# RWKV-5 attention into a top-1 mixture of experts: moving a count, an early block and the first load

## The chip, the cores and the metric

The kernel runs on one core of one Trainium2 chip. The metric is device microseconds for one execution. Before the change three executions took 365.10, 365.97 and 366.94 us; the median is 365.97 us. One more execution was taken with the hardware profiler on; it took 372.31 us, of which 370.4 us lie between its first and last instruction (the span). Every duration and waiting time below is from that execution.

## The reference

Two blocks follow each other. The first is a linear-attention recurrence (RWKV-5) over batch 4, 8 heads, 768 tokens and head width 48, with a decay `w` and a bonus `u` for each channel:

```
for t in range(S):
    cur = outer(u * k[t], v[t])
    y[t] = r[t] @ (state + cur)
    state = w[:, None] * state + outer(k[t], v[t])
```

The second takes the 3072 tokens of width 384 that result and sends each to one of 8 experts:

```
logits = x @ w_gate;  e = argmax(logits);  g = max of softmax(logits)
out = g * (relu(x @ w1[e]) @ w2[e])          # w1: 384 x 1024, w2: 1024 x 384
```

All values are float32.

## The kernel before

**Turns.** The attention works on pairs of heads: 4 batches of 4 pairs make 16 turns (`U`), numbered 0 to 15. In a turn the 768 tokens stand as 6 chunks (`G`) of 128 (`C`). r and k of a pair (`rk`) lie with the channels on 112 partitions, v and k once more (`vk`) with the tokens on 128. The instructions of every engine stand in the order in which the code records them; no scheduler moves them.

**A turn on TensorE.** `p_own` multiplies r by k by `u` for each token (into the tile `dsb`), `p_scores` makes the scores within the chunks (into `X`), `p_tr` transposes the outputs of the turn two before, `p_ds` makes each chunk's contribution to the state (also into `dsb`), and `p_out` of the turn before applies scores and states to v (into `yps`).

**A turn on the other engines.** VectorE turns the own terms round (`own_t`, line 295), scales r and k of the next pair by the decays (`scale`, line 272, into `RK`), masks the scores (`mask`) and carries the state over the chunks (`scan`, line 331). ScalarE writes the own terms on the diagonals of the score tiles (`diag`) and empties PSUM (`out_t`, line 356, into `yT`; `keep`, lines 369 and 370, into `xb`). POOL (GpSimd) multiplies r by k of the next pair (`pairs`, line 278, into `rp`) and k by its decay (`keys`), and sends finished tokens to their experts' rows in HBM by indirect DMAs (`send`, line 418). SP issues the loads; its queue takes them in order.

**Ahead of turn 1.** Pairs 0 to 2 are loaded at once. r and k of pair 0 come in one DMA of 112 partitions (line 95), are scaled in one instruction, multiplied in `pairs(0)` on VectorE, and only then come `p_own(0)` and what hangs on it. TensorE fills its waiting time with products of the identity that nobody reads (`p_fill`, line 115): 17 at the very start and 8 ahead of turn 1. A float32 product is two records in the profile.

**The count.** From turn 5 on, `choose`, `p_rank` and `slots` find the experts and places of a finished batch's tokens. In turn 12 `p_count` (line 429) adds up the tokens of each expert so far, as one small product into `dsb`; `count` (line 432) and a compare (line 752) then check that the first two experts have at least 160 tokens (`EARLY`). Before the change they stand between `p_own` and `own_t`, and between `own_t` and `scale`.

**After the last turn.** The first 160 rows of experts 0 and 1 (`early`) need no more of the last batch. Their first layer, `L1` (line 485), is eight blocks of three products; each is followed on ScalarE by a relu and, where `then` names one, by the issue of a weight load. Blocks of `early[0]` stand between the remaining steps of turns 14 and 15: two blocks, then `p_tr(14)`, `p_out(15)`, one block, `p_tr(15)` and `keep(15)`, `choose` of the last batch, three blocks, `p_rank` of the last batch (lines 391 to 394), and then the rest without a break. After that come the late passes over all experts, which load their rows only when the last tokens have been sent.

Of the kernel before, what the change touches and what calls it, by code (L numbers as in the profile page):

```python
# [13 lines left out]
ALU = mybir.AluOpType  # L14
# [4 lines left out]
B, H, S, D = 4, 8, 768, 48  # L19
# [4 lines left out]
C = 128  # L24
G = S // C
# [4 lines left out]
KP = 64 + D  # L30
# [6 lines left out]
EARLY = 160  # L37
# [3 lines left out]
def bc(ap, shape):  # L41
    return ap.to_broadcast(shape)


def straight(tc, rk, vk, w, w1, w2, out, flag):
# [8 lines left out]
    nc = tc.nc  # L54
# [8 lines left out]
    X01 = [pp.tile([128, 4, C], FP32, name=f"X{i}") for i in range(2)]  # L63
    X23 = pp.tile([128, 2, 512], FP32, name="X23")
    yps = [pp.tile([128, 512], FP32, name=f"yps{k}") for k in range(2)]
# [5 lines left out]
    hbank = [X01[0].rearrange("p a b -> p (a b)"), X23[:, 0, :], X01[1].rearrange("p a b -> p (a b)"), X23[:, 1, :]]  # L71
# [16 lines left out]
    rks = [ca.tile([128, 2, S], FP32, name=f"rk{i}") for i in range(3)]  # L88
    vks = [ca.tile([128, 2 * G - 1, 2 * D], FP32, name=f"vk{i}") for i in range(4)]

    def load_rk(i):
        if i < U:
            b, hp = divmod(i, HP)
            if i < 3:
                nc.sync.dma_start(rks[i % 3][0:KP], rk[b, hp].rearrange("h p u s -> (h p) u s")[0:KP])
            else:

                for h in range(2):
                    nc.sync.dma_start(rks[i % 3][64 * h:64 * h + D], rk[b, hp, h, 0:D])

    def load_vk(i):
        if i < U:
            b, hp = divmod(i, HP)
            nc.sync.dma_start(vks[i % 4], vk[b, hp])
# [7 lines left out]
    def p_fill(n, o):  # L112

        for _ in range(n):
            nc.tensor.matmul(o, lhsT=ident, rhs=ident, start=True, stop=True, skip_group_check=True)
# [8 lines left out]
        nc.sync.dma_start(rows.rearrange("(e n) c -> e (n c)", e=E)[e:e + 2, PAD * HP * Q:CAP * HP * Q].rearrange(  # L124
            "e (p z) -> p e z", p=128), bc(zt[:, None, :], [128, 2, nz]))

    p_fill(17, X01[1][:, 0, :])
    strict = cp.tile([128, C], FP32, name="strict")
    nc.gpsimd.memset(strict, 1.0)
    nc.gpsimd.affine_select(out=strict, in_=strict, pattern=[[1, C]], base=-1, channel_multiplier=-1,  # L130
# [4 lines left out]
    TT = cp.tile([KP, HP, 2, C], FP32, name="TT")  # L135
# [11 lines left out]
    def decays(h0, nh):  # L147


        m = C // 2  # L150
        nc.gpsimd.memset(two(h0, nh, m, C + m - 1, 1), 1.0)
        for l in range(7):
            nc.gpsimd.tensor_tensor(pw[:, l + 1, :], pw[:, l, :], pw[:, l, :], op=ALU.mult)
        for l in range(6):
            n = 1 << l
            nc.vector.tensor_tensor(two(h0, nh, m + n, C + m - 2 * n, n), two(h0, nh, m, C + m - n, n),
                                    bc(pw[:, l, h0:h0 + nh, None, None], [KP, nh, 2, n]), op=ALU.mult)
        nc.vector.reciprocal(inv, pw[:, 6, :])
        nc.vector.tensor_tensor(two(h0, nh, 0, C + m, m), two(h0, nh, m, C, m),
                                bc(inv[:, h0:h0 + nh, None, None], [KP, nh, 2, m]), op=ALU.mult)  # L160
# [23 lines left out]
    def state_decay():  # L184
        nc.gpsimd.memset(dec, 0.0)
        nc.gpsimd.tensor_copy(dec[:, :, :, 1:], bc(pw[:, 7, :, None, None], [KP, HP, D, G - 2]))
# [55 lines left out]
    cnt2 = cp.tile([128, E], FP32, name="cnt2")  # L242
# [5 lines left out]
    viol = cp.tile([128, 24], FP32, name="viol")  # L248


    RKs = [ca.tile([128, 2, S], FP32, name=f"RK{i}") for i in range(3)]
# [15 lines left out]

        return c + 4 * h if c < 4 else 8 + 2 * h + c - 4

    def scale(i):  # L270
        hp, x = i % HP, rks[i % 3]
        nc.vector.tensor_tensor(RKs[i % 3][0:KP].rearrange("p u (c t) -> p u c t", t=C),  # L272
                                x[0:KP].rearrange("p u (c t) -> p u c t", t=C),
                                bc(TT[:, hp, :, None, :], [KP, 2, G, C]), op=ALU.mult)

    def pairs(i, eng=None):
        x = rks[i % 3]
        (eng or nc.gpsimd).tensor_tensor(rps[i % 2][0:KP], x[0:KP, 0], x[0:KP, 1], op=ALU.mult)  # L278
# [6 lines left out]
    def p_own(i):  # L285


        hp = i % HP
        x = rps[i % 2][0:KP].rearrange("p (c a j) -> p a c j", a=4, j=32)
        for a in range(4):  # L290
            nc.tensor.matmul(dsb[32 * a:32 * a + 2, 240:240 + 32 * G].rearrange("p (c j) -> p c j", j=32),
                             lhsT=ubs[:, hp, :], rhs=x[:, a], start=True, stop=True, skip_group_check=True)

    def own_t(i):
        nc.vector.transpose(own[i % 2].rearrange("p c m -> p (c m)"), dsb[:, 240:240 + 32 * G])  # L295

    def p_scores(i, cs):
        r = RKs[i % 3]
        for c in cs:
            for h in range(2):  # L300
                q = slice(64 * h, 64 * h + D)
                o = X01[h][:, c, :] if c < 4 else X23[:, h, (c - 4) * C:(c - 3) * C]
                nc.tensor.matmul(o, lhsT=r[q, 1, c * C:(c + 1) * C], rhs=r[q, 0, c * C:(c + 1) * C],  # L303
                                 start=True, stop=True, skip_group_check=True)
# [24 lines left out]
    def scan(i):  # L329
        hp = i % HP  # L330
        nc.vector.tensor_tensor_scan(Ss[i % 2][0:KP].rearrange("p e g -> p (e g)"),
                                     dec[:, hp].rearrange("p e g -> p (e g)"), dsb[0:KP, 0:240], 0.0,
                                     ALU.mult, ALU.add)
# [33 lines left out]
    def keep(i):  # L367
        b, hp = divmod(i, HP)
        nc.scalar.copy(xbs[b % 3][:, 0:4, hp, :], trv[0])
        nc.scalar.copy(xbs[b % 3][:, 4:G, hp, :], trv[1])  # L370
# [26 lines left out]
    def slots(b):  # L397
        oh, xb = ohs[b % 2], xbs[b % 3]
        nc.vector.tensor_tensor(rko, rp, oh, op=ALU.mult)
        with nc.allow_low_precision("whole numbers below 2^24"):  # L400
            nc.vector.tensor_reduce(slot[b % 2], rko, axis=AX, op=ALU.add)
# [26 lines left out]
    def p_count():  # L428
        nc.tensor.matmul(dsb[:, 480:480 + E], lhsT=ones, rhs=osum, start=True, stop=True, skip_group_check=True)

    def count(dst):
        nc.vector.tensor_tensor(dst, dsb[:, 480:480 + E], basef, op=ALU.subtract)
# [267 lines left out]
    early = [Pass(e, 0, EARLY, 0, early_bufs[e]) for e in range(2)]  # L700
# [8 lines left out]

    selection()  # L710
    decays(0, HP)
    scale(0)
    pairs(0, nc.vector)
    key_decay(0, HP)
    state_decay()
    p_scores(0, range(2))
    p_own(0)
    own_t(0)
    p_key_decay(0, 1)
# [16 lines left out]
    mask(0, 1)  # L736
    p_scores(0, range(4, G))
    mask(0, 2)
    p_fill(8, yps[0][:, 384:512])
    load_vk(3)  # L740
    for i in range(1, U):
        b, k = divmod(i - 6, 4)
        rt = i >= 6 and k == 0 and b < B - 1
        if i == 1:
            load_rk(4)
        p_own(i)
        if i == 12:
            p_count()
        own_t(i)
        if i == 12:  # L750
            count(cnt2)
            nc.vector.tensor_scalar(out=viol[:, 12:14], in0=cnt2[:, 0:2], scalar1=float(EARLY), scalar2=None, op0=ALU.is_lt)
        if i > 1:
            nc.gpsimd.tensor_copy(turn, own[i % 2][0:1, 0, 0:1])
        behind = i > 6 and i % 4 == 3
        p_scores(i, range(4 if behind else G))
        if i + 1 < U:
            scale(i + 1)
            if i == 1:
                nc.gpsimd.tensor_copy(turn, RKs[2][0:1, 0, 0:1])  # L760
            pairs(i + 1)
            load_rk(i + 4)
            keys(i + 1, nc.vector if i in (7, 8, 11, 12) else None)
        if i == 3:
            numbers()
        if i == 5:
            more_numbers()
        diag(i)
        mask(i, 0)
        mask(i, 1)  # L770
        if 2 <= i:
            p_tr(i - 2)
        p_ds(i)
        if rt:
            p_rank(b)
            slots(b)
        scan(i)
        if behind:
            p_scores(i, range(4, G))
        if rt:  # L780
            mask(i, 2)
        if 2 <= i:
            keep(i - 2)
        if not rt:
            mask(i, 2)
        if i == U - 1:
            for p in early:
                p.xT()
        if rt:
            gates(b)  # L790
            total(b, nc.gpsimd)
            ids(b)
        if i in sends:
            send(*sends[i])
        p_out(i - 1)
        out_t(i - 1)
        if i % 4 == 1 and i > 4:
            choose((i - 5) // 4)
        load_vk(i + 3)
        if 2 <= i < 6:  # L800
            clear(2 * i - 4)
        if i == 12:
            weights1(0, (0, 1))
        if i == 13:
            for p in early:
                p.load()
        if i == 14:
            weights1(0, (2, 3))


    ends = [hbank[k] for k in (0, 2, 0, 2)]
# [4 lines left out]
    send(B - 2, range(3, G))  # L816
    p_out(U - 1)
    out_t(U - 1)
    early[0].L1(range(2, 3), bank=ends, then=[(weights1, 1, 2)])
    p_tr(U - 1)  # L820
    keep(U - 1)
    choose(B - 1)
    gates(B - 1)
    ids(B - 1)
    early[0].L1(range(3, 6), bank=[hbank[k] for k in (0, 1, 0, 2)], then=[(weights1, 1, 3), (weights2, 0, 0), (weights2, 0, 1)])
    p_rank(B - 1)
    slots(B - 1)
    send(B - 1, range(G))
# [646 lines left out]
```

## Time and profile before

| What | Value |
|---|---|
| Median of three executions | 365.97 us |
| Profiled execution | 372.31 us |
| Its span | 370.4 us |
| TensorE busy | 356.1 us, 96% |
| VectorE busy | 263.4 us, 71% |
| POOL busy | 204.7 us, 55% |
| ScalarE busy | 142.4 us, 38% |
| Start of turn 1, 2, 12, 13 and 14 on TensorE (`p_own`) | 18.40, 23.50, 87.42, 94.75, 100.97 us |
| First product of the early blocks | 114.14 us |
| First product of the late blocks | 148.61 us |

PE is TensorE's matmul side, PEld its weight loading, DVE is VectorE, ACT ScalarE, SP SyncE. Times are microseconds from the first instruction. In a bracket at the end of a line stands how long the engine had been idle before it, and what ended that wait. PEclk is the share of the full clock that TensorE was granted. The start of the span, up to turn 1, holds 18 us; the turns go to 114 us; the rest belongs to the experts.

### The profile page before, as it was taken

How to read it: one execution, taken by the hardware profiler on the slowest of the kernel's cores; microseconds unless marked ns; L12 is line 12 of the kernel's file. 1: busy time of each engine (PE TensorE's matmuls, PEld its weight loads, DVE VectorE, ACT ScalarE, POOL GpSimd, SP SyncE). 2: the span in 40 equal slices, each digit the busy share in tenths (PEclk: the TensorE clock that was granted, in tenths of full speed). 3: DMA queues.
4: the chain of work that ended last, by engine and by line, in shares of the span. 5: the costliest groups of instructions: out<-in, count | busy, mean ns of one | idle time of the engine just before them, and what ended most of it. 6: DMA issues, size and time to landing. Idle time of an engine off the chain costs nothing.

```text
span 370.4 us, 9106 instructions
## 1 busy us (share of the span) xinstructions
PE 356.1 (96%) x3355; PEld 336.8 (91%) x3355; DVE 263.4 (71%) x653; ACT 142.4 (38%) x411; POOL 204.7 (55%) x242
## 2 busy tenths in 40 slices
PE   6999999999899999999999999999999999999991
PEld 6788888888787899999999999999999999999891
DVE  5787887896873317694797996798788788765531
ACT  2487877976884320232222312221230321113210
POOL 5367888988964450372214606913931950999341
PEclk9699999999999999999999999999999999999998
DMA  7999987898746695778748416733842853313401
GB/s 200 243 204 218 249 256 193 242 238 199 248 101 222 197 365 150 188 208 245 190 151 203 125 62 193 190 104 99 217 147 104 188 163 117 119 50 85 145 18 51
DMA packets 35253, 63.81 MB, mean 172 GB/s; under 512 B 18873, under 2 KB 19913, under 8 KB 35200
## 3 DMA queue, kind: packets, MB, share of 16 engines
q1 hardware_dynamic: 29696, 48.59, 51.1%
q0 software_dynamic: 3776, 9.84, 7.7%
q10 hardware_dynamic: 1728, 4.72, 3.7%
q8 instruction: 28, 0.46, 0.5%
q14 instruction: 25, 0.20, 0.2%
HBM read 52.02 MB, written 11.40 MB: 171 GB/s over the span
## 4 chain that ended last, share of the span: by engine, by line
PE 81%; DMA 9%; POOL 4%; DVE 2%; issue 2%; SPq 0%; POOLq 0%; ACT 0%; DVEq 0%
PE X L507 12%; PE X L569 10%; PE yps L611 8%; PE X L485 8%; PE tr L611 8%; DMA rk<-in_rk_dram 6%; PE yps L507 5%; PE dsb L611 4%; PE X L303 4%; PE tr L507 3%; PE dsb L507 3%; POOL rp L278 3%; PE tr L364 3%; DMA vk<-in_vk_dram 3%; PE yps L346 3%; PE yps L569 2%
## 5 line engine op out<-in xcount | busy, mean ns | idle before, releaser
L684 POOL DMA_INDIRECT out_dram<-yo,ix x28 | 28.4, 1014 | 68.1 <-DVE so L629 43.1
L309 ACT ACTIVATE A<-ident,own 128x128 f32<-128x128 f32 x192 | 57.9, 389 | 12.1 <-DVE own L295 10.1
L418 POOL DMA_INDIRECT rows<-xb,slot x24 | 29.7, 1236 | 12.7 <-issue 5.1
L569 PE MATMUL X<-hT,w2s 128*128 128x160 f32 (+5 forms) x288 | 36.5, 287 | 0.0
L569 PEld LDWEIGHTS X<-hT,w2s 128*128 128x128 f32 x288 | 36.2, 191 | 0.2
L611 PE MATMUL yps<-tums,sums 128*128 128x192 f32 x184 | 32.4, 326 | 0.0
L303 PEld LDWEIGHTS X<-RK 48*128 48x128 f32 x384 | 23.5, 190 | 7.6 <-issue 4.8
L611 PEld LDWEIGHTS yps<-tums,sums 128*128 128x128 f32 x184 | 30.3, 190 | 0.0
L303 PE MATMUL X<-RK 48*128 48x128 f32 x384 | 27.6, 286 | 2.2 <-DVE RK L272 2.2
L278 POOL TENSOR_TENSOR rp<-rk 112x768 f32<-112x768 f32 x15 | 29.4, 1958 | 0.0
L272 DVE TENSOR_TENSOR RK<-rk,TT 112x1536 f32<-112x1536 f32 x16 | 27.6, 1724 | 2.3 <-DMA rk<-in_rk_dram 2.3
L684 POOL DMA_INDIRECT out_dram<-yt,it x16 | 16.8, 1049 | 20.5 <-DVE so L629 9.3
L315 DVE COPY_PREDICATED A<-strict,X 128x512 f32<-128x512 int32 x32 | 23.1, 740 | 4.6 <-ACT A L309 4.6
L507 PE MATMUL X<-xT,w1s 128*128 128x208 f32 (+5 forms) x120 | 26.0, 331 | 0.0
L698 POOL TENSOR_TENSOR tums<-w2s,tums 128x384 f32<-128x384 f32 x24 | 24.7, 1030 | 0.4
L346 PE MATMUL yps<-A,vk 128*48 128x128 f32 x384 | 24.0, 274 | 0.0
L507 PEld LDWEIGHTS X<-xT,w1s 128*128 128x128 f32 x120 | 20.9, 190 | 0.0
L346 PEld LDWEIGHTS yps<-A,vk 128*48 128x48 f32 x384 | 20.2, 123 | 0.5
L364 PE MATMUL tr<-sel,yT 112*128 112x104 f32 x128 | 18.5, 287 | 1.4 <-ACT yT L356 0.8
L640 ACT ACTIVATE so<-so,xg 128x192 f32<-128x192 f32 x24 | 10.0, 450 | 25.2 <-DVE so L629 21.8
L611 PE MATMUL tr<-w2s,hT 128*128 128x192 f32 x112 | 19.4, 326 | 0.0
L645 ACT COPY so<-tr 128x192 f32<-128x192 f32 x7 | 2.2, 320 | 44.4 <-PE tr L611 44.4
(214 smaller groups left out, 835.6 us busy)
## 6 DMA issues: line engine op xcount, KB each, us to landing
w1s<-in_w_dram SPq DMA_DIRECT2D x36, 384.0 KB
w2s<-in_w_dram SPq DMA_DIRECT2D x24, 384.0 KB
vk<-in_vk_dram SPq DMA_DIRECT2D x16, 528.0 KB
rk<-in_rk_dram SPq DMA_DIRECT2D x26, 288.0 KB
w2s<-in_w_dram ACTq DMA_DIRECT2D x8, 384.0 KB
xs<-rows SPq DMA_DIRECT2D x16, 169.0 KB
rk<-in_rk_dram SPq DMA_DIRECT2D x3, 672.0 KB
w1s<-in_w_dram ACTq DMA_DIRECT2D x4, 384.0 KB
```

The costliest lines, as they stand in the source:

```text
L272: nc.vector.tensor_tensor(RKs[i % 3][0:KP].rearrange("p u (c t) -> p u c t", t=C), x[0:KP].rearrange("p u (c t) -> p u c t", t=C), bc(TT[: ...
L278: (eng or nc.gpsimd).tensor_tensor(rps[i % 2][0:KP], x[0:KP, 0], x[0:KP, 1], op=ALU.mult)
L303: nc.tensor.matmul(o, lhsT=r[q, 1, c * C:(c + 1) * C], rhs=r[q, 0, c * C:(c + 1) * C], start=True, stop=True, skip_group_check=True)
L309: nc.scalar.activation(A[:, place(c, h), :], ident, func=ACT.Copy, scale=own[i % 2][:, c, h:h + 1])
L346: nc.tensor.matmul(o(c, h), lhsT=v[:, c, h * D:(h + 1) * D], rhs=A[:, place(c, h), :], start=c < 2, stop=c == 0, skip_group_check=True)
L364: nc.tensor.matmul(trv[c // 4][:, c % 4, :], lhsT=yTs[i % 3][0:KP, c & 1, (c // 2) * C:(c // 2 + 1) * C], rhs=sel[:, c & 1, i % HP, :], st ...
L418: s_ = nc.gpsimd.indirect_dma_start(out=rows[:, :], out_offset=bass.IndirectOffsetOnAxis(ap=slot[b % 2][:, c:c + 1], axis=0), in_=xbs[b % ...
L485: nc.tensor.matmul(p[:, 0:self.n], lhsT=w1s[self.k % 2][f // 2][:, m, f % 2 * 128:(f % 2 + 1) * 128], rhs=self.t[:, m, 0:self.n], start=m ...
L507: nc.tensor.matmul(p[:, at * n:(at + 1) * n], lhsT=a, rhs=b, start=j == 0, stop=j == len(ab) - 1, skip_group_check=True)
L569: nc.tensor.matmul(p[:, 0:n], lhsT=w2s[self.k % 2][f // 2][:, f % 2, m * 128:(m + 1) * 128], rhs=self.h[:, f, self.c:self.n], start=f == 0 ...
L611: nc.tensor.matmul(p[:, at * Z:(at + 1) * Z], lhsT=a(f), rhs=b(f), start=f == 0, stop=f == FT // 2 - 1, skip_group_check=True)
L684: s_ = nc.gpsimd.indirect_dma_start(out=to[:, :], out_offset=bass.IndirectOffsetOnAxis(ap=at, axis=0), in_=x, in_offset=None, bounds_check ...
```

## The change

Three places change; what is computed stays the same.

- The first r, k come in two DMAs, chunks 0 to 2 and chunks 3 to 5, and are scaled in two instructions. The scores of the first two chunks move from behind `pairs`, `key_decay` and `state_decay` to directly behind the first scaling, and five fillings follow them. The first row of fillings falls from 17 to 12, the one ahead of turn 1 from 8 to 6.
- In turn 12 `p_count` moves behind `p_ds`, just ahead of the scan; `count` and the compare move behind the scan.
- After `p_out(15)` two early blocks stand ahead of `p_tr(15)` instead of one, and two instead of three behind it. Each block takes its weight load with it.

```
@@ load_rk
             if i < 3:
-                nc.sync.dma_start(rks[i % 3][0:KP], rk[b, hp].rearrange("h p u s -> (h p) u s")[0:KP])
+                for q in (slice(0, S // 2), slice(S // 2, S)) if not i else (slice(0, S),):
+                    nc.sync.dma_start(rks[i % 3][0:KP, :, q], rk[b, hp].rearrange("h p u s -> (h p) u s")[0:KP, :, q])
...
-    p_fill(17, X01[1][:, 0, :])
+    p_fill(12, X01[1][:, 0, :])
...
-    def scale(i):
+    def scale(i, c0=0, c1=G):
         hp, x = i % HP, rks[i % 3]
-        nc.vector.tensor_tensor(RKs[i % 3][0:KP].rearrange("p u (c t) -> p u c t", t=C),
-                                x[0:KP].rearrange("p u (c t) -> p u c t", t=C),
-                                bc(TT[:, hp, :, None, :], [KP, 2, G, C]), op=ALU.mult)
+        nc.vector.tensor_tensor(RKs[i % 3][0:KP].rearrange("p u (c t) -> p u c t", t=C)[:, :, c0:c1],
+                                x[0:KP].rearrange("p u (c t) -> p u c t", t=C)[:, :, c0:c1],
+                                bc(TT[:, hp, :, None, :], [KP, 2, c1 - c0, C]), op=ALU.mult)
...
     decays(0, HP)
-    scale(0)
+    scale(0, 0, G // 2)
+    p_scores(0, range(2))
+    p_fill(5, X23[:, 0, 0:C])
+    scale(0, G // 2, G)
     pairs(0, nc.vector)
     key_decay(0, HP)
     state_decay()
-    p_scores(0, range(2))
     p_own(0)
...
-    p_fill(8, yps[0][:, 384:512])
+    p_fill(6, yps[0][:, 384:512])
...
         p_own(i)
-        if i == 12:
-            p_count()
         own_t(i)
-        if i == 12:
-            count(cnt2)
-            nc.vector.tensor_scalar(out=viol[:, 12:14], in0=cnt2[:, 0:2], scalar1=float(EARLY), ...)
...
+        if i == 12:
+            p_count()
         scan(i)
+        if i == 12:
+            count(cnt2)
+            nc.vector.tensor_scalar(out=viol[:, 12:14], in0=cnt2[:, 0:2], scalar1=float(EARLY), ...)
...
-    early[0].L1(range(2, 3), bank=ends, then=[(weights1, 1, 2)])
+    early[0].L1(range(2, 4), bank=ends, then=[(weights1, 1, 2), (weights1, 1, 3)])
     p_tr(U - 1)
     keep(U - 1)
     choose(B - 1)
     gates(B - 1)
     ids(B - 1)
-    early[0].L1(range(3, 6), bank=[hbank[k] for k in (0, 1, 0, 2)], then=[(weights1, 1, 3), (weights2, 0, 0), (weights2, 0, 1)])
+    early[0].L1(range(4, 6), bank=[hbank[k] for k in (0, 1, 0, 2)], then=[(weights2, 0, 0), (weights2, 0, 1)])
     p_rank(B - 1)
```

More of the change, by code (lines that the diff above doesn't have):

```diff
@@ L746, in straight @@
         p_own(i)
-        if i == 12:
-            p_count()
         own_t(i)
-        if i == 12:
-            count(cnt2)
-            nc.vector.tensor_scalar(out=viol[:, 12:14], in0=cnt2[:, 0:2], scalar1=float(EARLY), scalar2=None, op0=ALU.is_lt)
         if i > 1:
@@ L776, in straight @@
             slots(b)
+        if i == 12:
+            p_count()
         scan(i)
+        if i == 12:
+            count(cnt2)
+            nc.vector.tensor_scalar(out=viol[:, 12:14], in0=cnt2[:, 0:2], scalar1=float(EARLY), scalar2=None, op0=ALU.is_lt)
         if behind:
```

## The prediction

> **What bounds the kernel now.** I read the page first. TensorE is busy for 96% of the span, and the chain that ended last is TensorE for 81%, so an edit counts only if it moves TensorE. In the second row below the granted clock falls to 0.6 in the second of 40 slices (9.3 to 18.5 us).
>
> ```profile
> PE   6999999999899999999999999999999999999991
> PEclk9699999999999999999999999999999999999998
> ```
>
> Next I read the busy time by windows, cut where the clock changes. Columns: stretch, its length, then busy time (records) of PE, PEld, DVE, ACT, POOL, then clock, DMA share, GB/s.
>
> ```profile
> 5.19:8.60 3.41, 2.09 (x19) 1.89 (x17) 1.40 (x2) 0.00 (x0) 1.72 (x11) 1.00 1.03 260
> 8.60:12.02 3.42, 2.25 (x26) 1.43 (x27) 3.12 (x5) 0.67 (x3) 0.00 (x0) 1.00 1.05 256
> 12.02:15.43 3.41, 3.41 (x34) 2.82 (x35) 3.07 (x4) 3.36 (x12) 0.99 (x2) 0.50 1.01 249
> 15.43:18.84 3.41, 3.41 (x23) 2.85 (x21) 1.36 (x3) 0.00 (x0) 2.13 (x2) 0.50 1.07 226
> 18.84:25.66 6.82, 6.69 (x129) 5.56 (x122) 6.18 (x8) 5.59 (x18) 4.20 (x4) 1.00 1.02 203
> ```
>
> TensorE is two thirds busy up to 12.02, and is then held at half clock for 6.82 us. The DMA engines are full throughout. Then the timeline, at the three places that the change touches (columns: start, busy us, engine, line, operation, and in brackets the idle time before it with what ended it). The start:
>
> ```profile
> 7.71 1.76 DVE L272 TENSOR_TENSOR RK<-rk,TT 112x1536 f32<-112x1536 f32 x1 [2.01 <-DMA rk<-in_rk_dram]
> 9.52 0.72 PE L303 MATMUL X<-RK 48*128 48x128 f32 x8 [2.25 <-DVE RK L272]
> 10.39 0.51 PE L291 MATMUL dsb<-rp,wug 112*2 112x192 f32 x8 [0.15 <-DVE rp L278]
> 14.69 3.78 PE L115 MATMUL yps<-ident 128*128 128x128 f32 x16
> 18.40 0.69 PE L291 MATMUL dsb<-rp,wug 112*2 112x192 f32 x8
> ```
>
> The first r, k ends a wait of VectorE and, through it, of TensorE; the 8 fillings run back to back into turn 1 at 18.40. Turn 12, with the count:
>
> ```profile
> 89.93 0.38 DVE L295 STREAM_TRANSPOSE own<-dsb 128x192 f32<-128x192 f32 x1 [2.75 <-PE X L303]
> 90.59 3.91 POOL L278 TENSOR_TENSOR rp<-rk 112x768 f32<-112x768 f32 x1
> 94.75 0.51 PE L291 MATMUL dsb<-rp,wug 112*2 112x192 f32 x8 [0.94 <-DVE S L331]
> ```
>
> The transpose of the own terms comes 2.5 us after its matmuls (87.42), and the next turn then waits 0.94 us. The end of the turns:
>
> ```profile
> 122.05 0.86 ACT L356 COPY yT<-yps 112x384 f32<-112x384 f32 x2 [2.97 <-PE X L485]
> 122.58 1.30 PE L364 MATMUL tr<-sel,yT 112*128 112x104 f32 x8 [0.58 <-issue]
> 126.51 0.21 DVE L384 TENSOR_TENSOR oh<-eq,m 128x48 bf16<-128x48 f32 x1
> 126.77 0.18 PE L392 MATMUL dsb<-oh,tri 128*128 128x48 bf16 x1
> ```
>
> **What the Trainium skill says.** "TensorE: Matmul & The Clock Gate", Part 1, "What's actually happening": the clock is half or full, set by how busy the array was in a free-running window of about 3.4 us. The steps at 12.02 and 18.84 lie two such windows apart, which agrees; where the windows fall differs by run. "DMA: Bandwidth & Descriptors", "Queues, rings and completion order": each engine takes descriptors in ring order. The trace's landings agree: rk0 7.62, vk0 9.57, rk1 12.59, vk1 14.43, vk2 20.12, rk3 23.27. The same page, "Specifications", puts line rate at pieces of 512 B and more; halves cut the pieces from 6144 to 1536 B, and no run here shows that size. "GPSIMD Engine Reference", "Specifications": its SBUF interfaces are shared with VectorE. The trace agrees: the product on POOL takes 3.91 us beside VectorE's scaling, 1.81 us elsewhere.
>
> **Step 1, halves.** Before: rk0 lands, scaling 7.71 to 9.47, product (0.95 us, the row of 112x768) to 10.34, p_own(0) at 10.39. After: the first half is scaled early, and when the second has landed only half a scaling is left, also 112x768, so about 0.95. The landing can move from 7.7 (same bytes, engines full) to 8.5 (smaller pieces); I take 7.9. Then 7.9 + 0.95 + 0.95 = 9.8, so 0.6 us earlier (0 to 0.8). SP's extra issue, 0.42 us, stands ahead of vk0, rk1 and the rest; those queue behind full engines, so I take 0.2 us at most for them.
>
> **Step 2, fillings, 25 to 23.** The first 12 end near 6.0 (0.44 us each until 5.19, then about half); the two scores wait for VectorE until about 7, so nothing waits for these. The five behind the scores stand ahead of p_own(0): from 7.1 they take 1.2 us at full clock or 2.3 at half, ending at 8.4 or 9.5, before 9.8: hidden, barely. The last six: p_own(0) to the first p_ds is 2.17 us of handovers (10.39 to 12.56), so p_ds moves to 11.95; from there to the fillings 2.13 us; then six at 3.78 / 8 = 0.47 us, 2.8 us, ending at 16.9 against 18.4. The product of pair 1 on POOL (16.39 before, up to 16.6) is just behind that cover. So turn 1 starts 1.5 us earlier. But the clock stays at half until 18.84 by the same windows: 1.94 us of turn 1 run there instead of 0.44, and the extra 1.5 us do 0.75 us of work. Kept: 0.75. What is late next: scaling of pair 3 (24.38) has 1.1 us over its landing, which holds 0.75.
>
> **Step 3, the count.** p_count, the count and the compare leave the place ahead of own_t and scale, and stand behind p_ds and the scan. In the trace TensorE's semaphore steps for the own terms at 89.15 and for the count at 89.83: 0.69 us. Scaling starts 0.55 us after own_t there, 0.31 in turn 2: 0.24 more. So pairs(13) moves by 0.69, from an end of 94.50 to 93.8; the scan by 0.93, from 94.61 to 93.7. TensorE was free at 94.75 - 0.94 = 93.81. Added: the count (0.13) now carries the semaphore that p_own(13) waits for, so 93.8, and behind it only the last mask is 0.3 us later, for which the scores wait not before 1 us into the turn. Gain 0.75. Ends: if the late semaphore is not the count's doing, only the 0.24 stays; at best the 1.1 us by which turn 12 (7.33) exceeds turn 13 (6.22).
>
> **Step 4, the early block.** A block is 6 records, 0.82 us (18 in 2.47). Put ahead of p_tr(15), it covers the 0.58 us in which that waits for yT; p_tr(15) starts at 122.82, 0.24 later. But the block is missing behind it: p_tr ends at 124.57, the one-hot follows 2.4 us later (124.33 to 126.72 before), at 126.97, while two blocks last to 126.2. So 0.75 us of new idle for 0.58 removed, and ScalarE's relu and weight issue of that block now stand ahead of keep(15). Net 0.3 later. Ends: -0.2 if the yT wait is longer in other runs; +0.8 if yT is released only when the longer run of blocks has ended. The weight load moves with its block; the rows of the last tokens, later by 0.3 us, have about 2 us before the first late block at 148.47.
>
> **Sum.** -0.75 - 0.75 + 0.3 = -1.2 us: the profiled execution from 372.31 to 371.1 (span 370.4 to 369.2). It runs 6.3 us above the median of the unprofiled runs, 365.97, so I carry the difference over: 364.8. About 0.5%, or 1.8 us, is what a measurement can tell from no change.
>
> **Rivals.**
> A. The clock is not lowered at all. For it: the five new fillings lie in the gap that 5.19 to 12.02 shows. Against: the last window before 12.02 loses the first scores. TensorE then waits for pairs(1) at 16.6 and runs turn 1 at full clock: 1.8 + 0.2 instead of 0.75, total -2.45: 363.5.
> B, slower. The clock is not given back at 18.84. Its place is the window from 15.43: it was all fillings, and would now hold fillings to 16.9 and then p_own and scores. For it: 12.02 to 15.43 was 100% busy with small matmuls and was not enough. Against: from 18.84 on the turns' own matmuls keep it. One window more is 3.41 us at half clock, 1.7 us; two are 3.4. With the other steps +0.5 to +2.2: 366.5 to 368.2. It decides from the point where the extra half-clock time passes 2.4 us, twice the 1.2 gained.
> C. The start gives nothing, because runs without the profiler already have full clock there; then pairs(1) sets turn 1 and rk1 comes up to 0.2 us later. 0 to +0.2, -0.75, +0.3: 365.6.
>
> **How the numbers follow.** Forecast 0.40 (its own range 364.0 to 365.9, from the ends of steps 3 and 4), A 0.25, B 0.17, C 0.18. Of the forecast a quarter, and of A nearly all, lies below 364.1; of B about half, and of C and the forecast a trace, above 367.8. That gives faster 0.34, same 0.55, slower 0.11. The range 363.1 to 367.1 leaves out a tail of A and the upper half of B.
>
> **What would show it.** Step 1: p_own(0) near 9.8. Step 2: p_own(1) near 16.9, clock 0.5 between about 12 and 19. Step 3: own_t(12) under 1.9 us behind its matmuls, p_own(13) without a wait. Step 4: no wait ahead of p_tr(15), but one of 0.7 ahead of the rank. I am wrong if the half clock lasts past 20 us, or if own_t(12) is as late as before.

## The result, and the profile after

The change made the kernel slower: 370.94 us against 365.5 us in the first comparison (medians of 5 executions each), a ratio of 1.0135 with a 95% interval of 1.0108 to 1.0163. In a later comparison the medians were 370.55 (19 executions) and 365.88 (54). Five of those 19 lie 1.5% or more above the fastest and are left out of the ratio; the median of the other 14 is 369.91. The ratios in this document are not the quotients of the medians. The prediction was 364.8, with a range up to 367.1.

The profiled execution of the changed kernel took 369.27 us (span 367.4), three microseconds *less* than the profiled one of before (372.31, span 370.4). So the two profiles can't explain a loss of 5 us. The kernel before was therefore run once more, with spans and clocks (e0 below): its profiled execution took 365.10 us, span 363.2, like its median. That is the execution to compare with; the differences between the three are the main finding.

One row of the two pages shows the granted clock of TensorE in 40 slices of the span. First the repeated kernel before, whose clock dips in no slice but the last:

```profile
PEclk9999999999999999999999999999999999999997
```

Then the changed kernel: the clock is a tenth lower in the third slice (18.4 to 27.6 us).

```profile
PEclk9989999999999999999999999999999999999998
```

Busy time by windows, counted in steps of 3.41 us from the first point at which each trace tells its clock (7.52 and 5.71 us; columns as in the prediction: stretch, length, busy time of PE, PEld, DVE, ACT, POOL, then clock, DMA share, GB/s). The repeated before:

```profile
7.52:10.93 3.41, 2.88 (x33) 1.97 (x31) 3.12 (x5) 0.45 (x3) 0.00 (x0) 1.00 1.01 259
10.93:14.35 3.42, 3.42 (x49) 3.01 (x46) 3.42 (x5) 3.42 (x13) 1.18 (x2) 1.00 1.04 289
14.35:17.76 3.41, 3.00 (x60) 2.35 (x60) 3.20 (x4) 1.77 (x7) 1.93 (x2) 1.00 1.05 265
```

The changed kernel:

```profile
12.54:15.95 3.41, 1.84 (x18) 1.52 (x14) 2.30 (x3) 1.66 (x6) 0.48 (x2) 1.00 1.02 244
15.95:19.36 3.41, 1.89 (x32) 1.52 (x32) 3.18 (x6) 0.90 (x4) 2.62 (x2) 1.00 1.04 246
19.36:22.77 3.41, 3.41 (x48) 3.14 (x44) 3.31 (x5) 2.71 (x10) 2.45 (x3) 0.50 1.04 240
```

TensorE is 84% busy or more in each window of the first, and keeps its clock. In the second it is busy for 54% and 55% of two windows in a row, and the third runs at half clock, in the middle of turn 1. The timeline shows what it waited for. The repeated before (start, busy us, engine, line, operation, and in brackets the idle time with what ended it):

```profile
6.85 1.76 DVE L272 TENSOR_TENSOR RK<-rk,TT 112x1536 f32<-112x1536 f32 x1 [1.15 <-DMA rk<-in_rk_dram]
9.53 0.51 PE L291 MATMUL dsb<-rp,wug 112*2 112x192 f32 x8 [0.15 <-DVE rp L278]
11.35 1.76 DVE L272 TENSOR_TENSOR RK<-rk,TT 112x1536 f32<-112x1536 f32 x1
12.70 2.05 PE L115 MATMUL yps<-ident 128*128 128x128 f32 x16
15.16 0.51 PE L291 MATMUL dsb<-rp,wug 112*2 112x192 f32 x8 [0.41 <-POOL rp L278]
```

The changed kernel:

```profile
5.83 2.45 DVE L274 TENSOR_TENSOR RK<-rk,TT 112x768 f32<-112x768 f32 x2
9.21 0.51 PE L293 MATMUL dsb<-rp,wug 112*2 112x192 f32 x8 [0.34 <-DVE rp L280]
12.77 1.60 PE L117 MATMUL yps<-ident 128*128 128x128 f32 x12
13.65 1.76 DVE L274 TENSOR_TENSOR RK<-rk,TT 112x1536 f32<-112x1536 f32 x1 [2.16 <-DMA rk<-in_rk_dram]
17.47 0.51 PE L293 MATMUL dsb<-rp,wug 112*2 112x192 f32 x8 [3.09 <-POOL rp L280]
```

Pair 0 is 0.3 us earlier (9.21 against 9.53), but the scaling of pair 1 waits 2.16 us for its r, k, which it had not done in the repeated before (it started at 11.35, just behind the work ahead of it on VectorE). The fillings end at 14.37, and TensorE then stands idle for 3.09 us until the product of pair 1 on POOL is done.

Turn 12, the repeated before, with the count in its old place:

```profile
84.42 0.38 DVE L295 STREAM_TRANSPOSE own<-dsb 128x192 f32<-128x192 f32 x1 [1.06 <-PE dsb L429]
90.03 0.51 PE L291 MATMUL dsb<-rp,wug 112*2 112x192 f32 x8
```

And the changed kernel, behind the scan:

```profile
92.33 0.14 DVE L434 TENSOR_TENSOR cnt<-dsb,basef 128x8 f32<-128x8 f32 x1
93.84 0.51 PE L293 MATMUL dsb<-rp,wug 112*2 112x192 f32 x8
```

Before, turn 12 runs from 83.70 to 90.03, 6.33 us; after, from 87.38 to 93.84, 6.46 us. There was hardly anything to gain here: the 7.33 us of turn 12 in the profile that the prediction read do not occur. The end of the turns, the repeated before:

```profile
114.82 0.86 ACT L356 COPY yT<-yps 112x384 f32<-112x384 f32 x2 [1.82 <-PE yps L351]
115.75 1.04 PE L364 MATMUL tr<-sel,yT 112*128 112x104 f32 x8
119.57 0.18 PE L392 MATMUL dsb<-oh,tri 128*128 128x48 bf16 x1
119.72 8.40 PE L485 MATMUL X<-xTe,w1s 128*128 128x160 f32 x60
```

The changed kernel:

```profile
118.63 0.86 ACT L358 COPY yT<-yps 112x384 f32<-112x384 f32 x2 [1.82 <-PE yps L353]
120.38 1.04 PE L366 MATMUL tr<-sel,yT 112*128 112x104 f32 x8
124.01 0.18 PE L394 MATMUL dsb<-oh,tri 128*128 128x48 bf16 x1 [0.47 <-DVE oh L386]
124.16 4.05 PE L487 MATMUL X<-xTe,w1s 128*128 128x160 f32 x28
```

With one early block ahead of them the last turned tokens do not wait in the repeated before (no bracket at 115.75): one block already covers the copy of yT. The second block pushes them back by its own length, and the rank then waits 0.47 us. From the last p_out's second half (114.00 and 117.82) to the block behind the rank it takes 5.72 us before and 6.34 after: 0.62 lost.

The difference between the two spans lies in these places:

| place | repeated before | changed | lost, us |
|---|---|---|---|
| p_own(1) starts | 15.16 | 17.47 | 2.31 |
| turn 1 lasts | 4.90 | 6.28 | 1.38 |
| turn 12 lasts | 6.33 | 6.46 | 0.13 |
| last p_out to the block behind the rank | 5.72 | 6.34 | 0.62 |
| sum; next block starts | 119.72 | 124.16 | 4.44 |
| span | 363.2 | 367.4 | 4.2 |

Two limits of this comparison. The changed kernel's profiled execution is the fastest of its six (369.27; the others took 370.76 to 371.18 at a mean clock of 0.985 to 0.988 instead of 0.991), so the table holds 4.2 of the 5.4 us between the medians. One more window at half clock, as e1 below has, would lower the mean clock by about that much, but those executions have no trace. And the repeated before has the earliest p_own(1) of all traces: the same start in e2 and e3 below began turn 1 at 15.49 and 15.72, so 0.3 to 0.6 of the 2.31 us is the luck of that execution.

The profile that the prediction started from differs from the repeated one at its own places: 3.44 us up to p_own(2) (23.50 and 20.06), 1.28 in turns 2 to 12, 1.37 from there to the last p_out, and 1.11 around the rank. That is 7.2 us, its whole excess in span (370.4 and 363.2). The part behind the start is not an accident of one execution: it comes back in e8 to e11 below, on another chip.

### The profile page after: what moved, and what is told of

Its sections match the earlier page's. It is cut to its first block, busy times and chain, and to the rows that moved or that the text cites. A ratio compares the mean times of both kernels' runs of the same rounds, so it can differ in the third digit from the quotient of the medians.

```text
span 367.4 us, 9100 instructions
## 1 busy us (share of the span) xinstructions
PE 353.5 (96%) x3351; PEld 335.3 (91%) x3351; DVE 264.9 (72%) x654; ACT 142.8 (39%) x411; POOL 205.4 (56%) x242
## 3 DMA queue, kind: packets, MB, share of 16 engines
q0 software_dynamic: 3776, 9.84, 7.6%
## 4 chain that ended last, share of the span: by engine, by line
PE 92%; DMA 3%; DVE 1%; POOL 1%; SPq 1%; ACT 0%; issue 0%; POOLq 0%; DVEq 0%
PE X L509 12%; PE X L571 10%; PE yps L613 8%; PE X L487 8%; PE tr L613 8%; PE X L305 6%; PE yps L348 6%; PE yps L509 5%; PE tr L366 5%; PE yps L353 4%; PE dsb L613 4%; PE tr L509 3%; PE dsb L509 3%; DMA rk<-in_rk_dram 3%; PE dsb L328 2%; PE yps L571 2%
## 5 line engine op out<-in xcount | busy, mean ns | idle before, releaser
L420 POOL DMA_INDIRECT rows<-xb,slot x24 | 33.8, 1408 | 12.2 <-issue 4.5
L274 DVE TENSOR_TENSOR RK<-rk,TT 112x1536 f32<-112x1536 f32 (+1 forms) x17 | 28.2, 1658 | 2.3 <-DMA rk<-in_rk_dram 2.2
L280 POOL TENSOR_TENSOR rp<-rk 112x768 f32<-112x768 f32 x15 | 27.2, 1816 | 0.0
L348 PE MATMUL yps<-A,vk 128*48 128x128 f32 x384 | 25.2, 283 | 0.0
L348 PEld LDWEIGHTS yps<-A,vk 128*48 128x48 f32 x384 | 21.4, 128 | 0.6
L700 DVE TENSOR_TENSOR quart<-w1s 128x128 f32<-128x128 f32 x69 | 19.2, 285 | 0.0
```

The source lines that it names most:

```text
L348: nc.tensor.matmul(o(c, h), lhsT=v[:, c, h * D:(h + 1) * D], rhs=A[:, place(c, h), :], start=c < 2, stop=c == 0, skip_group_check=True)
L420: s_ = nc.gpsimd.indirect_dma_start(out=rows[:, :], out_offset=bass.IndirectOffsetOnAxis(ap=slot[b % 2][:, c:c + 1], axis=0), in_=xbs[b % ...
L700: (eng or nc.vector).tensor_tensor(o, a, b, op=how)
```

## The experiments

Three theories stood at the start. K, the clock: the change leaves TensorE idle at the start, so that its clock is lowered in executions in which the kernel before keeps it. L, the load: smaller pieces delay all later transfers. D: the loss lies in a later part. All times are medians; "low" counts executions with a mean clock under 0.992, which is about where one stretch of 3.41 us at half clock puts it. It is a rough cut: the profiled execution of f3 has such a stretch and counts 0.992.

**The parts one by one.** e0 is the kernel before. e1 has the start alone: the load and scaling in halves and the fillings 12, 5, 6.

> The kernel before, unchanged, to have its spans and granted clocks beside its times. Theory K (the clock; the profiled execution of before, 372.31 us, was not typical): executions near 365.5 us keep the full clock through the start or lose it for one stretch of 3.4 us at most, mean clock 0.990 or more, and p_own(1) starts near 17 us. Theory D (the profile was typical in the start, and the change loses elsewhere): half clock from about 12 to 18.8 us again, mean clock 0.986, and the 6 us between profile and median lie in the stages behind the turns.

> The first r, k in halves, the five fillings moved behind the first scores and the last fillings cut from 8 to 6, with the count and the early block as before. Theory K: nearly all of the loss is here, 4.5 to 6 us slower than before (370 to 371.5), mean clock down by about 0.005 to 0.008, the half clock coming in the first turns after the 3 us in which TensorE waits for the product of pair 1. Theory L (the load: smaller pieces delay rk1 and all later loads): also slower here, but with the clock as before and with waits on transfers of 3 us or more in the turns. Theory D: within 0.7 us of before.

The count alone:

```
-        if i == 12:
-            p_count()
         own_t(i)
...
+        if i == 12:
+            p_count()
         scan(i)
+        if i == 12:
+            count(cnt2)
```

> Only the token count of turn 12 moved behind the scan. Theories K and L: 0 to 1.1 us faster than before. Theory D: this part or the next carries the loss, 2 us slower or more.

The early block alone:

```
-    early[0].L1(range(2, 3), ...)
+    early[0].L1(range(2, 4), ...)
...
-    early[0].L1(range(3, 6), ...)
+    early[0].L1(range(4, 6), ...)
```

> Only the early block moved ahead of the last turned tokens. Theories K and L: from 0.2 us faster to 0.8 us slower. Theory D: this part or the count carries the loss, 2 us slower or more, seen as waits between 110 and 150 us.

| kernel | us | before on that chip | ratio, 95% interval | low |
|---|---|---|---|---|
| e0 before | 365.76 | 366.06 | 0.9997 [0.9975, 1.0019] | 5 of 20 |
| e1 start | 369.54 | 366.06 | 1.0080 [1.0059, 1.0101] | 19 of 20 |
| e2 count | 365.90 | 366.06 | 1.0003 [0.9981, 1.0026] | 4 of 20 |
| e3 early block | 367.01 | 366.06 | 1.0015 [0.9989, 1.0041] | 6 of 20 |

The kernel before itself was low in 19 of 71. Theory K holds for the place: the start carries most of the loss, and its clock is lowered nearly always instead of in about one execution of four. The size is 3.5 us, under the 4.5 to 6 that K asked for. TensorE's wait behind the late r, k of pair 1 is there too, so K and L were not yet told apart; D falls. The windows of e1:

```profile
13.19:16.60 3.41, 1.05 (x10) 0.85 (x8) 2.61 (x3) 1.03 (x4) 0.79 (x2) 1.00 1.01 202
16.60:20.01 3.41, 2.20 (x21) 1.55 (x22) 2.44 (x5) 0.89 (x3) 2.32 (x2) 0.50 1.04 216
20.01:23.42 3.41, 3.41 (x46) 3.17 (x46) 3.41 (x5) 2.73 (x10) 2.02 (x3) 0.50 1.03 212
```

One window with TensorE 31% busy, then two at half clock. Its p_own(1) starts at 17.81, 2.65 us after e0's, and its turn 1 lasts 7.26 us, 2.36 longer: 5.0 in all, and its span is 4.9 longer (368.1). The count moves nothing that can be measured; its trace has turn 12 at 6.46 us, 0.13 longer, as in the changed kernel. The early block's interval includes no change (0.95 us in the medians); its trace has the same 6.34 us around the rank.

**What in the start.** e4 takes the halved transfer out of e1, e5 has it alone, e6 is e1 with 18 fillings ahead of turn 1 instead of 6, and e7 is before with 12 and 6 fillings instead of 17 and 8.

```
 e4    fillings and scaling of e1, load of before
 e5  + for q in (slice(0, S // 2), slice(S // 2, S)) if not i else (slice(0, S),):
 e6  - p_fill(6, yps[0][:, 384:512])
     + p_fill(18, yps[0][:, 384:512])
 e7  - p_fill(17, X01[1][:, 0, :])        - p_fill(8, yps[0][:, 384:512])
     + p_fill(12, X01[1][:, 0, :])        + p_fill(6, yps[0][:, 384:512])
```

> The start as changed (scaling in halves, fillings 12, 5, 6), but the first r, k in one transfer as before. Theory H (the halved transfer is what costs: all loads behind it land later, rk1 near 13.8 us instead of 11.3, so turn 1 starts 2.3 to 2.7 us later, and that wait of TensorE then brings the half clock): rk1 lands near 11.5 again, p_own(1) starts near 15.2, and the time is 365.3 to 366.8, at the full clock in most executions. Theory F (the fewer fillings are what costs, whatever the load): 368 to 369.5 and a mean clock of 0.987 in most executions.

> Only the first r, k loaded in two transfers; scaled whole, fillings 17 and 8 as before. Theory H: rk1 lands at 13 us or later, p_own(1) starts 2 us or more later than the 15.16 of the repeated before, the clock is lowered in most executions, 368 to 370. Theory F: 365.3 to 366.5.

> The start as changed, with 18 fillings instead of 6 behind the last scores of pair 0: 12 more of 0.26 us each cover the 3.1 us in which TensorE waits for the product of pair 1. If the half clock comes from that idle time, the clock stays full through turns 1 and 2, turn 1 lasts 5 us again instead of 6.3 to 7.3, and what stays is the late start alone: p_own(1) near 17.6 and a time 2 to 2.5 us over before, 367.8 to 368.5. If the clock is lowered for another reason, 369.5 as without the added fillings, or more.

> The kernel before with 12 instead of 17 fillings at the start and 6 instead of 8 ahead of turn 1, and nothing else changed. Theory H: within 0.7 us of before (365.5 to 366.8), with at most a few more executions at the lower clock. Theory F: 368 or more, at a mean clock of 0.987.

Before took 365.96 here, low in 13 of 46.

| kernel | us | ratio, 95% interval | low | rk1 landed | p_own(1) |
|---|---|---|---|---|---|
| e4 | 368.36 | 1.0062 [1.0039, 1.0085] | 19 of 20 | 11.15 | 15.38 |
| e5 | 368.59 | 1.0070 [1.0038, 1.0102] | 8 of 11 | 13.61 | 17.54 |
| e6 | 370.93 | 1.0131 [1.0072, 1.0191] | 2 of 4 | 12.52 | 16.54 |
| e7 | 368.08 | 1.0042 [1.0024, 1.0059] | 20 of 20 | 11.85 | 17.48 |

Neither theory wins: the halved transfer alone costs 2.6 us, the fewer fillings alone 2.1, and each is enough to have the clock lowered in most executions. They don't add: e1 loses 3.5, not 4.7. In the trace of e5 the clock fell at 11.61, behind a wait of 1.80 us for the first scores and before the late r, k of pair 1 (13.61) were waited for. The windows of e7 show the second way. The 12 fillings end by 6.8 us, and nothing runs on TensorE until the scores at 9.11:

```profile
6.62:10.03 3.41, 0.99 (x14) 0.60 (x17) 2.74 (x3) 0.00 (x0) 0.25 (x8) 1.00 1.02 282
10.03:13.45 3.42, 3.42 (x31) 2.08 (x33) 2.84 (x4) 2.24 (x9) 0.00 (x0) 0.50 1.04 274
```

e4 got its r, k of pair 1 in time (p_own(1) at 15.38), yet its clock was low as often as e1's. In its profiled execution the clock fell at 23.54, in turn 2, behind a wait of TensorE of 1.30 us for which the profile names no cause. Turn 2 took 11.05 us there instead of 6.22, which is its whole loss of span, so this trace does not show how fewer fillings cost. e6 kept the full clock in the profiled execution and its turn 1 lasted 4.91 us, as expected of the cover; but that execution took 367.98, and the three others 369.38 to 372.69. Turns 3 and 4 were 0.24 and 1.17 us longer there than in e0, with POOL waiting 1.8 us for v, k. Cover alone does not bring the time back, and I have no full account of it.

**Two transfers, or small pieces? And which fillings?** e8 is before with the first r, k in two transfers by rows (64 and 48), so that the pieces stay at 6144 B. e9, e10 and e11 are before with other numbers of fillings at the start and ahead of turn 1.

```
 e8  - nc.sync.dma_start(rks[i % 3][0:KP], ...[0:KP])
     + for p in (slice(0, 64), slice(64, KP)) if not i else (slice(0, KP),):
     +     nc.sync.dma_start(rks[i % 3][p], ...[p])
 e9    fillings 12 and 8      e10   17 and 6      e11   22 and 8
```

> The kernel before with the first r, k loaded in two transfers that part the 112 rows (64 and 48) and keep the pieces at 6144 B. Theory I (the second transfer as such costs: the sync engine issues all that follows 0.9 to 1.1 us later, and the loads behind it fall back): rk1 lands at 12.8 us or later, and the time is 368 to 370, as with the halved load alone. Theory P (the small pieces of 1536 B cost): rk1 lands at 11.2 to 12.2, first to last of its 16 shares within 2.2 us, and the time is 365.4 to 366.8.

> The kernel before with 12 fillings at the start instead of 17. Theory S (the fillings at the start decide: they end before the first scores can start, TensorE then idles and the clock is lowered): nearly all executions at a mean clock of 0.987, about 368. Theory E (those ahead of turn 1 decide): as before, 365.3 to 366.5, about a quarter of the executions at the lower clock.

> The kernel before with 6 fillings instead of 8 ahead of turn 1. Theory S: as before, 365.3 to 366.5, about a quarter of the executions at the lower clock. Theory E: nearly all executions at a mean clock of 0.987, about 368.

> The kernel before with 22 fillings at the start instead of 17. Theory S: the share of executions at the lower clock falls from about a quarter to under a tenth, and the highest times near 368 go; median 365.3 to 366.3, the upper end where the first scores wait up to 1 us for the last fillings in executions whose clock is granted late. Theory E: a quarter of the executions at the lower clock as before.

They ran on a chip on which before took 371.05 us (low in 18 of 59), so only comparisons within this table count.

| kernel | us | ratio, 95% interval | low |
|---|---|---|---|
| e8 two transfers by rows | 373.10 | 1.0036 [1.0011, 1.0061] | 14 of 20 |
| e9 12 and 8 | 374.28 | 1.0113 [1.0087, 1.0139] | 4 of 4 |
| e10 17 and 6 | 372.57 | 1.0021 [0.9996, 1.0046] | 11 of 20 |
| e11 22 and 8 | 371.79 | 1.0013 [0.9987, 1.0038] | 7 of 22 |

e8 is right for theory P in the transfers and wrong in the time. Its rk1 landed at 11.80 (the three others on that chip: 11.22 to 11.81), the first of its 16 shares at 10.95: a spread of 0.85 us. In the traces with 1536 B pieces rk1 landed at 13.62 (changed), 13.97 (e1), 13.61 (e5), with spreads of 3.1 to 3.4 us, and at 11.66 to 12.52 with 1.8 to 2.4 in e6, f2 and f3. The sync engine of e8 too issued the loads behind later than in e0 (rk1 at 2.96 and 2.20; 3.30 with halves), so most of that delay and the second transfer as such do not explain the late landings; that points to the pieces, on one trace of e8. Over all traces rk1 landed at 11.66 to 13.97 with halves (six traces, mean 13.0) and at 11.15 to 12.59 with one transfer (ten, mean 11.7). But the last row of r, k 0 itself landed at 7.75 instead of 6.92 to 7.15 (e9 to e11), p_own(0) started at 10.56, and TensorE waited 2.85 us for the first scores; the clock then was at half from 11.09 to 17.92. A late first pair costs as well as a late second one. On the fillings, 12 at the start are too few (e9, four executions only) and 6 ahead of turn 1 are doubtful (e10), while 22 at the start are no better than 17 (e11), against theory S; neither S nor E holds alone. (One execution of e10, of 2046 us, and one of e11, of 733, hardly move the medians.)

These four traces also bear on the profile that the prediction read. Turn 12 took 7.46 to 7.48 us in all four and 7.33 there, against 6.33 or 6.46 in the twelve other traces; around the rank it was 6.9 to 7.2 and 6.83, against 5.71 to 6.34. All four have the code of before in both places, and e10 shows the late transpose, 2.6 us behind p_own(12) (85.31):

```profile
87.94 0.38 DVE L295 STREAM_TRANSPOSE own<-dsb 128x192 f32<-128x192 f32 x1 [2.78 <-PE X L303]
```

So the waits that steps 3 and 4 of the prediction priced do exist, on a chip on which the kernel before is 5 us slower. Which chip that first profile came from is not on record. Neither the moved count nor the early block was run on the slower chip, so what they would gain there stays open.

All 17 traces together show how the fillings and the clock act on each other at the start. When TensorE is first granted its full clock differs between executions of one kernel (5.19 and 7.52 us in the two of before), and the earlier that is, the earlier the 17 fillings end (7.28 and 8.38). In the five traces in which TensorE then waited 1.80 us or longer for the first scores (before, e5, e7, e8, e9) the clock was lowered between 10.03 and 12.02; in the twelve with 1.52 us or less it was not lowered there. Twelve fillings ended by 6.93 us in every trace, but the first scores came by 7.97 where the scaling was halved and only at 9.00 and 9.11 where it was not (e9, e7). This may be why before is low in about one execution of four and e7 in all. It is not shown: most executions have no trace, and e11, whose 22 fillings last beyond the start of the scores (9.57 and 9.50), was low in 7 of 22.

**Putting both back, and the early block in the changed kernel.** f1 is e1 with one transfer and 17 and 8 fillings: of the changed start, only the scaling in halves and the five fillings are left. f2 is the changed kernel with the early block back in its old place, f3 the changed kernel.

```
 f1    load of before; scale(0) in halves; fillings 17, 5, 8
 f2  - early[0].L1(range(2, 4), ...)
     + early[0].L1(range(2, 3), ...)
     - early[0].L1(range(4, 6), ...)
     + early[0].L1(range(3, 6), ...)
```

> The start as changed, but with both suspects undone: the first r, k in one transfer of 6144 B pieces, and 17 and 8 fillings instead of 12 and 6 (the five behind the first scores stay, as does the scaling in halves). If these two are the whole of what the start loses: 365.3 to 366.8 on a chip where before takes 366.0, about a quarter of the executions at the lower clock, rk1 landing near 11.3. If scaling in halves or the five fillings cost by themselves: 367.5 or more.

> The changed kernel with the early block back behind the last turned tokens. If that block costs there what it costs alone (1.0 us in the mean of the run with this part alone, 0.6 us in its trace): 0.6 to 1.0 us faster than the changed kernel of this call, 3.4 to 3.8 us slower than before. If all of the loss is the start's: the same as the changed kernel within 0.3 us.

> The changed kernel once more, for the clocks of more executions: 4.3 to 5.0 us slower than before, at a mean clock of 0.991 or less in nine of ten executions or more.

| kernel | us | ratio to before (365.88), 95% interval | low |
|---|---|---|---|
| f1 | 365.84 | 0.9990 [0.9969, 1.0011] | 1 of 20 |
| f2 | 369.62 | 1.0079 [1.0057, 1.0102] | 16 of 20 |
| f3 | 370.55 | 1.0082 [1.0051, 1.0112] | 14 of 19 |

With the transfer and the fillings put back, the start loses nothing. f1's windows hold 87% or more of busy TensorE, with most of the five fillings in the first of them:

```profile
6.30:9.71 3.41, 3.09 (x29) 2.78 (x29) 2.60 (x3) 0.00 (x0) 0.81 (x10) 1.00 1.04 283
9.71:13.13 3.42, 3.42 (x53) 2.41 (x52) 3.07 (x5) 2.26 (x8) 0.00 (x0) 1.00 1.02 266
13.13:16.54 3.41, 2.98 (x34) 2.46 (x34) 3.19 (x7) 1.84 (x7) 2.98 (x3) 1.00 1.04 262
```

Its clock was lowered in 1 execution of 20, where before had 16 of 54, but its executions at the full clock are no faster than before's (medians 365.75 and 365.56 at a mean clock of 0.992 or more), so the two times can't be told apart. The executions of f3 spread from 365.51 to 378.93; 14 of 19 are low, where nine of ten were expected. f2 against f3 does not settle the early block: 0.93 us in the medians, 0.3 when the five highest of f3 are left out, and the intervals of the ratios overlap. The traces give 0.62: 6.34 us around the rank in f3, 5.71 in f2. f3's profiled execution shows that even a landing in time is not enough with 6 fillings. Its rk1 landed at 11.66 and TensorE waited only 1.65 us ahead of turn 1:

```profile
13.65:17.06 3.41, 1.76 (x30) 1.25 (x30) 3.19 (x6) 0.98 (x4) 2.97 (x3) 1.00 1.07 281
17.06:20.48 3.42, 3.42 (x48) 3.17 (x46) 3.33 (x5) 3.06 (x11) 2.11 (x3) 0.50 1.02 157
```

Beside that, turns 3 and 4 of f3 took 7.58 and 7.14 us instead of 6.22 each, 2.3 us that the start does not hold. f2 lost 1.3 us in turns 3 to 7 and e6 1.4 in turns 3 and 4; e1, e5 and the first profile of the changed kernel lost 0.2 or nothing there. This part of the loss is not explained.

One execution of f3 took 365.51 at a mean clock of 0.996: the changed kernel can be as fast as before, it seldom is.

## Why the prediction was wrong

Two terms of the sum failed: the 0.2 us of step 1 for the loads behind the halves, and the cover of step 2. Steps 3 and 4 were sized on waits that the executions at the median do not have.

**The base.** The sum was made against one execution of 372.31 us, 6.3 over the median, and its difference carried over to the median. All that the steps set out to remove (the half clock of the start, the late transpose of turn 12, the wait for yT) was part of that excess, and absent from the execution of 365.10 us. The late transpose was there again in e8 to e11 and a wait ahead of p_tr(15) in e8 to e10 (0.62 to 0.66 us), on the slower chip; the half clock of the start comes in about one execution of four. None of them is in the repeated one. Rival C had the right premise, that runs at the median keep the clock at the start (by the mean clock 52 of 71), and drew too little from it: that the change could then *take* the clock away. The gap of 6.3 us was in hand, and it said that the profile was not of the executions to be predicted.

**Step 1, halves.** Predicted 0.6 us earlier for p_own(0), from 10.39 to 9.8; measured 9.21, against 9.53 in the repeated before and 9.84 and 9.85 in e3 and e2. Right for pair 0, and of no use: p_own(1) comes 3.84 us after rk1 lands (scaling 1.76, product 1.80, handovers) in e0, 3.85 in the changed kernel and in f3. What failed is the term "I take 0.2 us at most for them" for the transfers behind: rk1 landed 2.3 us later (13.62 and 11.32; 1.3 in the mean of all traces). The extra issue of 0.42 us, which was also in that term, was 0.93: vk0 was issued at 2.66 instead of 1.73. "DMA: Bandwidth & Descriptors" of the Trainium skill, "Specifications", puts full rate at pieces of 512 B and more. The rate of a piece does agree roughly: 1536 B took 0.091 us on average in e1 and 0.102 in f2, 6144 B 0.351 in e0 up to 14 us: 16.9, 15.1 and 17.5 B/ns. But the first piece started at 2.76 instead of 2.32, and the shares of the transfers behind came later. The rate of a piece says nothing on either.

**Step 2, fillings.** The mechanism was misplaced. The step expected half clock from 12.02 to 18.84 and fillings back to back up to 16.9; the fillings ran at full clock, in 1.60 us instead of 2.8, ended at 14.37, and nothing covered TensorE until the product of pair 1 was done. "Just behind that cover" was the term that failed: the product ended at 17.41, not 16.6, and the cover 2.5 us earlier than thought. With the clock lost behind that wait, a gain of 0.75 became a loss of 2.31 + 1.38.

**Step 3, the count.** Predicted -0.75, measured +0.13 in every trace with the moved count. The transpose came 0.73 us after the start of its matmuls in e0, not 2.5. (The step's own figures, 94.75 to 93.81, give 0.94, not 0.75; it does not say where the rest goes.)

**Step 4, the early block.** Predicted +0.3, measured +0.62 in the traces, and in the times nothing clear of the noise. The new idle time was there, if smaller (0.47 of wait for 0.75); the 0.58 removed did not exist.

**Rivals.** B named the right resource and a loss, at the wrong place: it wanted the clock lowered at 12.02 and not given back, and it came in the turns, after an idle stretch that B did not have. It also took only the clock's 1.7 to 3.4 us, without the late transfer. The sign the prediction named for itself, half clock past 20 us, is what the profile showed (19.36 to 22.77).

## What to carry to other kernels

Before pricing a change from a profile, ask whether the profiled execution is one of those that make the median; where it lies outside the range of the times, the waits in it may be the excess itself, and those of another chip. Work that only keeps TensorE busy is priced by the idle time that follows when it ends early, not by the time it takes: here five fillings less at the start and two less ahead of turn 1 cost 2.1 us in the median and left all 20 executions of e7 with a low mean clock. And in a stretch in which the transfers are the limit, what makes the first one useful earlier is worth nothing if the one behind it comes later.

## What the runs showed of the hardware

- Up to the end of the turns the clock was lowered in stretches of 3.41 or 6.83 us, which agrees with the windows that "TensorE: Matmul & The Clock Gate" of the Trainium skill describes (Part 1, "What's actually happening"). Windows 84% busy and more kept the clock (e0, f1); windows at 29% (e7), 31% (e1) and 52% (f3) were followed at once by half clock. In between the share alone did not decide: in the changed kernel one at 54% was not, and the next, at 55%, was; 66% in the first profile of before and 72% in e5 were, 65% in e2 was not. In e1 and e7 half clock went on for a second window although the first had TensorE busy for 64% and 100%.
- With the first transfer in 1536 B pieces, rk1 landed at 11.66 to 13.97 us in six traces, its 16 shares 1.8 to 3.4 us apart; in ten with one transfer of 6144 B pieces at 11.15 to 12.59, 1.5 to 2.8 apart; in e8 with two of 6144 B at 11.80, 0.85 apart. The ranges meet, so the three late ones (13.6 to 14.0) are not explained by the pieces alone. Why they come apart was not tried.
- Left open: the waits of TensorE of 1.1 to 1.3 us in turns 2 and 3 (e4, f3) for which the profile names no cause, the times of e6, the 1.3 to 2.3 us that e6, f2 and f3 lost in turns 3 to 7, and the early block in the times.
